# A guard on the weights that squares and sums every 16th column instead of all of them

## The chip, the core and the metric

The kernel runs on one core of a Trainium2 chip. The core has engines that run side by side, each through its own list of instructions in order: TensorE (PE in the profile) for matrix products, VectorE (DVE) and ScalarE (ACT) for work on tiles, GpSimd (POOL), and SyncE (SP), which here only issues DMAs. An engine that has to wait for another stands at a semaphore, and everything behind the waiting instruction in its list stands too. The metric is the device time of one execution in microseconds (us).

## What is computed

Two stages in a row. The first is a linear recurrence over 768 steps for 4 batches and 8 heads of width 48: a complex state, decayed by a gate of magnitude at most 0.999 at each step, takes up the outer product of k and v, and q reads it. The second takes the 3072 rows that come out (384 wide) through a two-layer network with 2048 hidden columns.

```python
mag = np.sqrt(a_re * a_re + a_im * a_im)
scale = np.minimum(mag, 0.999) / (mag + 1e-06)
a_re_n, a_im_n = (a_re * scale, a_im * scale)
for t in range(S):
    new_re = ar * S_re - ai * S_im
    new_im = ar * S_im + ai * S_re
    kv = np.einsum('bhd,bhe->bhde', k[:, :, t], v[:, :, t])
    S_re, S_im = (new_re + kv, new_im)
    y[:, :, t] = np.einsum('bhd,bhde->bhe', q[:, :, t], S_re)
...
h = x @ w_in
g = h - np.tanh(h)
return (g @ w_out).astype(np.float32)
```

## The kernel before

The sequence is cut into 6 chunks of 128 steps. A chunk of one batch is a unit (24 units), and two units are a group (12 groups, g = 0 to 11). For a group the kernel first computes the gates (`gates_b`, `gates_b2`, `gates_c`, `gates_d`, `gates_e`): logarithms and arctangents of the gate on ScalarE, sums over the 128 steps on TensorE (`cumsum`, lines 213 to 220), sines, cosines and exponentials on ScalarE. `products` (line 368) multiplies q and k with them (`qkf`, line 390), splits the result into a high and a low float16 part (`q`, `k`; the high part on ScalarE, line 400, the low part on VectorE, line 401) and transposes both by DMA (line 402). `attention` (line 424) makes the products within the chunk and with the carried state. The second stage works for a group as eight steps (fp = 0 to 7): `head` (line 513) has 18 matmuls into `h`, a tanh on ScalarE and a subtraction on VectorE into `mt`; `split` (line 531) makes a high part (ScalarE) and a low part (VectorE) of `mg`; `tail` (line 539) has 12 matmuls into `o`.

The arctangent in `gates_c` belongs to one set of ScalarE's function tables, logarithm and exponential to another, so each group loads tables (the rows named ACT_TABLE_LOAD, or ACT L102 with 1.28 us in the chain). After the arctangent, ScalarE writes the high part of the angle (`a_raw` in float16), and the first matmuls of `cumsum` (line 219) sum it.

The lists of the engines are not written out by hand. The strings START, FIRST, SECOND and CYCLE (lines 45 to 56) give the order in which the program's pieces are issued, for CYCLE in every group from g = 2; then a scheduler orders the instructions by priority and by its own estimate of when each can run and how long it takes. OFFSET and EARLY (lines 57 and 58) move the priority by kind. The guard's instructions have the kind "guard". Instructions of all helpers are recorded in `call` (line 102), so most rows of the profile have L102 and differ by their tile.

Beside the computation the kernel collects statistics that tell whether its fast path may be used (`stat`, line 131). For the weights it is `weight_stats` (line 193): for each of the 16 tiles of w_in and of w_out, one ScalarE instruction squares 384 columns of the high part and sums them per partition into a column of `stats`, and the square itself goes to a tile that nobody reads (`junk`). The sum is fetched by a second instruction, which the profile calls ACTIVATION_READ_ACCUMULATOR. The items w0 and w1 of SECOND and CYCLE call it, in `step` (lines 589 to 592). `check_stats` (line 556) compares all columns with limits at the end; they come from STAT_KINDS (line 70).

Of the kernel before, what the change touches and what calls it, by code (L numbers as in the profile page):

```python
# [13 lines left out]
AF = mybir.ActivationFunctionType  # L14
# [5 lines left out]
DM, DF = 384, 2048  # L20
# [5 lines left out]
FT = DF // P  # L26
# [47 lines left out]
    "o": (2 * NG - 2, -2.0 ** 100, 2.0 ** 100),  # L74
    "g": (FT // 2, 0.0, 2.0 ** 100),
    "x": (2 * NG, 14.0, 2.0 ** 30),
    "w": (2 * FT, 4.0, 2.0 ** 21.9),
}
STAT_COLS = {}
NSTAT = 0  # L80
# [6 lines left out]
def tile_fast(ctx: ExitStack, tc: tile.TileContext, flag, a_in, qkv_in, win_in, wout_in, sq_c, vec_c, lim_c, out):  # L87
    nc = tc.nc
    V, G, A, T, SP = nc.vector, nc.gpsimd, nc.scalar, nc.tensor, nc.sync
# [16 lines left out]
    V, G, A, T, SP = map(eng, (V, G, A, T, SP))  # L106
# [24 lines left out]
    def stat(kind, n=1):  # L131
        i = STAT_COLS[kind][used.count(kind)]
        used.extend([kind] * n)
        return stats[:, i:i + n]

    def junk():
        return sb.tile([P, 2 * HD], F16, name="junk")
# [32 lines left out]
    wi, wo = {}, {}  # L170
# [20 lines left out]
            combine("declo", "declo", out=t[:, 1], in0=w, in1=t[:, 0], op=ALU.subtract)  # L191

    def weight_stats(ft):
        A("guard").activation(out=junk()[:, :DM], in_=wi[ft][:, 0], func=AF.Square, accum_out=stat("w"))
        A("guard").activation(out=junk()[:, :DM], in_=wo[ft][:, 0], func=AF.Square, accum_out=stat("w"))


    gate = {}
# [382 lines left out]
    def step(g, x):  # L581
        kind, i = x[0], int(x[1:] or 0)
        if kind == "F":
            (gates_first, gates_second)[i]()
        elif kind == "q":
            load_qkv(i)
        elif kind in "io":
            decode(i, (0,) if kind == "i" else (1,))
        elif kind == "w":
            if 1 <= g <= FT // 2 and (kind, 2 * g + i) not in live:  # L590
                live[kind, 2 * g + i] = True
                weight_stats(2 * (g - 1) + i)
        elif kind in "pa":
            u = 2 * g + i
            if u < 2 * NG:
                advance(kind, u)
        elif g + i < NG and (kind, g + i) not in live:
            assert not any((kind, j) in live for j in range(g + i, NG))
            live[kind, g + i] = True
            steps[kind](g + i)  # L600
# [222 lines left out]
```

## Time and profile before

| what | value |
|---|---|
| runs without profile | 574.28, 575.5, 575.92 us; median 575.5 |
| profiled execution, own time | 575.09 us |
| its span, first to last instruction | 573.3 us |
| TensorE busy | 502.8 us, 88% of the span |
| VectorE busy | 475.2 us, 83% |
| ScalarE busy | 474.1 us, 83% |
| mean granted TensorE clock | 0.978 of full speed |

The span is shorter than the execution's own time by 1.8 us, which lie before its first and after its last instruction. The durations below come from this one execution. In the timelines a row has its start, its time, and in brackets the idle time before it with what ended it; an instruction on ScalarE or VectorE reaches some 0.1 us into the next one, so the distance between two starts is what it takes from its engine. In the chain of waits, each row is a piece of the time that ended last.

### The profile page before, as it was taken

Reading aid. Unit: us, or ns where it says so; the run is one execution under the profiler, and the core shown is the slowest. Engines: PE = TensorE matmul, PEld = TensorE weight load, DVE = VectorE, ACT = ScalarE, POOL = GpSimd, SP = SyncE. Lnnn points to the kernel's source line nnn. Section 1 sums busy time; section 2 is a strip of 40 time slices with the busy share of each in tenths; the row PEclk is TensorE's granted clock in tenths of the full one; section 3 lists DMA queues with packets and bytes.
Section 4 is the critical chain, followed back from the end, with each engine's and each line's share of the span. In section 5 each row is a group of like instructions: output and inputs, shape, how many; then the busy total and the mean of one; then the engine's idle time right before and its main releaser. Section 6 shows DMA issues by size and latency. Waiting matters only on the chain.

```text
span 573.3 us, 12669 instructions
## 1 busy us (share of the span) xinstructions
PE 502.8 (88%) x5058; PEld 385.8 (67%) x5058; DVE 475.2 (83%) x806; ACT 474.1 (83%) x951; POOL 2.3 (0%) x8
## 2 busy tenths in 40 slices
PE   2336499988879998999998999999999999999995
PEld 0135386856657766877776777778778777777773
DVE  4898899979799879898987998999998989853331
ACT  6978799897988978998988998998989989553551
POOL 1000000000000000000000000000000000000000
PEclk9998699999989999999998999999999999999999
DMA  7757834319675487176286285293482652720001
GB/s 248 212 167 173 267 111 125 112 20 203 120 125 145 74 129 172 45 147 154 56 153 143 49 183 143 59 182 106 99 179 67 136 110 57 147 58 15 4 25 33
DMA packets 133902, 68.12 MB, mean 119 GB/s; under 512 B 119982, under 2 KB 123694, under 8 KB 133836
## 3 DMA queue, kind: packets, MB, share of 16 engines
q1 hardware_dynamic: 133836, 67.25, 50.6%
q8 instruction: 41, 0.67, 0.5%
q14 instruction: 25, 0.20, 0.1%
HBM read 36.76 MB, written 4.78 MB: 72 GB/s over the span
## 4 chain that ended last, share of the span: by engine, by line
PE 34%; ACT 27%; DVE 22%; DMA 9%; issue 7%; SPq 1%; ACTq 0%; DVEq 0%
PE h L521 11%; PE o L548 10%; PE att L102 8%; ACT L102 5%; ACT a_raw L102 5%; DMA qT<-q 4%; DVE qkf L390 3%; DMA kT<-k 3%; DVE g_t L102 3%; ACT mg L102 3%; DVE qkv_raw L387 2%; DVE q L119 2%; ACT mt L102 2%; ACT g_t L102 2%; DVE mg L102 2%
## 5 line engine op out<-in xcount | busy, mean ns | idle before, releaser
L521 PE MATMUL h<-xT,w 128*128 128x256 f16 x1728 | 209.8, 275 | 13.5 <-DMA xT<-x 10.9
L548 PE MATMUL o<-w,mg 128*128 128x384 f16 x1152 | 204.3, 326 | 1.7 <-ACT mg L102 1.0
L521 PEld LDWEIGHTS <-w 128*128 128x128 f16 x1728 | 168.6, 99 | 43.9 <-DMA xT<-x 8.6
L548 PEld LDWEIGHTS <-mg 128*128 128x128 f16 x1152 | 111.3, 98 | 66.0 <-ACT mg L102 1.2
L102 DVE SCALAR_TENSOR_TENSOR mt<-h,mt 128x512 f32<-128x512 f32 x96 | 65.0, 688 | 28.6 <-ACT mt L102 27.7
L102 DVE SCALAR_TENSOR_TENSOR mg<-mt,mg 128x512 f16<-128x512 f32 x96 | 65.0, 687 | 17.4 <-ACT mg L102 16.5
L102 ACT ACTIVATE mt<-h 128x512 f32<-128x512 f32 x96 | 55.0, 587 | 24.5 <-PE h L521 24.4
L102 ACT ACTIVATE mg<-mt 128x512 f16<-128x512 f32 x96 | 59.1, 626 | 16.3 <-DVE mt L102 16.1
L102 ACT ACT_TABLE_LOAD x39 | 50.0, 1283 | 1.4 <-PEq L816 0.8
L102 PE MATMUL att<-qT,kT 96*128 96x128 f16 (+1 forms) x544 | 40.9, 228 | 4.1 <-DMA kT<-k 3.7
L390 DVE TENSOR_TENSOR qkf<-qkv_raw,g_trig 128x768 f32<-128x768 f32 x44 | 41.1, 952 | 0.0
L102 ACT ACTIVATE a_raw<-a_raw 128x768 f32<-128x768 f32 (+2 forms) x49 | 39.0, 798 | 0.5 <-DVE a_raw L102 0.4
L102 PEld LDWEIGHTS <-kT 96*128 96x128 f16 x480 | 29.3, 99 | 8.0 <-DMA kT<-k 4.6
L102 DVE TENSOR_TENSOR a<-af,a 128x512 f16<-128x512 f32 x40 | 27.2, 686 | 7.8 <-ACT a L102 7.7
L102 DVE TENSOR_TENSOR af<-att,sqc 128x512 f32<-128x512 f32 x40 | 27.3, 687 | 5.4 <-PE att L102 4.3
L102 ACT ACTIVATE a<-af 128x512 f16<-128x512 f32 x40 | 24.8, 623 | 3.7 <-DVE af L102 3.7
L102 DVE SCALAR_TENSOR_TENSOR g_t<-g_t,a_raw 128x768 f32<-128x768 f32 (+1 forms) x26 | 23.2, 897 | 2.3 <-ACT a_raw L102 2.3
L119 DVE TENSOR_TENSOR q<-qkf,q 128x768 f16<-128x768 f32 x20 | 19.1, 956 | 5.3 <-ACT q L102 5.3
L102 ACT ACTIVATE w<-wtmp 128x384 f16<-128x384 f32 x32 | 16.1, 518 | 8.4 <-DVE wtmp L186 8.4
L102 ACT ACTIVATE q<-qkf 128x768 f16<-128x768 f32 x20 | 16.9, 843 | 6.7 <-DMA qT<-q 6.4
L102 ACT ACTIVATE g_trig<-g_t 128x768 f32<-128x768 f32 (+1 forms) x26 | 20.4, 787 | 2.0 <-DVE g_t L102 2.0
L102 PE MATMUL att<-sqc,qkf 128*96 128x128 f32 x32 | 7.0, 386 | 16.2 <-DVE qkf L390 15.8
(94 smaller groups left out, 700.6 us busy)
## 6 DMA issues: line engine op xcount, KB each, us to landing
qkv_raw<-in_qkv SPq DMA_DIRECT2D x24, 576.0 KB
a_raw<-in_a SPq DMA_DIRECT2D x22, 384.0 KB
io<-in_win SPq DMA_DIRECT2D x16, 384.0 KB
io<-in_wout SPq DMA_DIRECT2D x16, 384.0 KB
out_dram<-io SPq DMA_DIRECT2D x24, 192.0 KB
a_raw<-in_a SPq DMA_DIRECT2D x4, 192.0 KB
xT<-x SPq DMA_TRANSPOSE x24
hd<-hscr SPq DMA_DIRECT2D x20, 3.0 KB
```

Of the source, the lines that this page charges most:

```text
L102: return f(*a, **k)
L119: by_name[ENGINE[which]](kind).tensor_tensor(**k)
L387: V("prod").scalar_tensor_tensor(out=x, in0=vw(e), scalar=E_MAX, in1=x, op0=ALU.min, op1=ALU.mult)
L390: V("prod").tensor_tensor(out=f, in0=x[:, :, None].broadcast_to([P, H, 2, D]), in1=tg[:, :, sl].rearrange("p r (h d) -> p h r d", d=D), op ...
L521: T("h").matmul(h_ps[:, j].rearrange("p (two t) -> p two t", two=2), lhsT=wi[ft][:, wp, kt * P:(kt + 1) * P], rhs=xT[:, :, xp, kt, :], sta ...
L548: T("o").matmul(o_ps[tt][:, :DM], lhsT=gg[:, gp, j * 256 + tt * P:j * 256 + (tt + 1) * P], rhs=wo[ft][:, wp], start=(ft == 0 and n == 0), ...
```

## The change

The two instructions of `weight_stats` read every 16th column of the tile, 24 instead of 384. The lower and the upper limit for these sums are divided by 16. The number of instructions stays the same.

```diff
@@ -74,7 +74,7 @@
     "o": (2 * NG - 2, -2.0 ** 100, 2.0 ** 100),
     "g": (FT // 2, 0.0, 2.0 ** 100),
     "x": (2 * NG, 14.0, 2.0 ** 30),
-    "w": (2 * FT, 4.0, 2.0 ** 21.9),
+    "w": (2 * FT, 4.0 / 16, 2.0 ** 17.9),
 }
@@ -191,8 +191,8 @@
     def weight_stats(ft):
-        A("guard").activation(out=junk()[:, :DM], in_=wi[ft][:, 0], func=AF.Square, accum_out=stat("w"))
-        A("guard").activation(out=junk()[:, :DM], in_=wo[ft][:, 0], func=AF.Square, accum_out=stat("w"))
+        A("guard").activation(out=junk()[:, :DM // 16], in_=wi[ft][:, 0].rearrange("p (n s) -> p n s", s=16)[:, :, 0], func=AF.Square, accum_out=stat("w"))
+        A("guard").activation(out=junk()[:, :DM // 16], in_=wo[ft][:, 0].rearrange("p (n s) -> p n s", s=16)[:, :, 0], func=AF.Square, accum_out=stat("w"))
```

Since the scheduler estimates the shorter instructions as shorter, it also puts other instructions in another order. ScalarE's list is shown where it works at the second unit of the group whose period runs from 302.6 to 343.9 us in the trace; `w_9` and `w_10` are weight tiles, `q` and `k` the high parts that line 400 writes.

```order
 L102 ACTIVATE junk,stats<-xf 128x384
 L102 ACTIVATE mt<-h 128x512 x2
-L102 ACTIVATE junk,stats<-w_9_719 128x384
-L102 ACTIVATE q_89<-qkf 128x8x96
-L102 ACTIVATE mg<-mt 128x512 x2
-L102 ACTIVATE junk,stats<-w_9_781 128x384
-L102 ACTIVATE mt<-h 128x512
-L102 ACTIVATE junk,stats<-w_10_431 128x384
-L102 ACTIVATE rawsq<-qkv_raw 128x144
-L102 ACTIVATE junk,stats<-w_10_912 128x384
+L102 ACTIVATE junk,stats<-w_9_719 128x24
+L102 ACTIVATE q_89<-qkf 128x8x96
+L102 ACTIVATE mg<-mt 128x512
+L102 ACTIVATE junk,stats<-w_9_781 128x24
+L102 ACTIVATE mg<-mt 128x512
+L102 ACTIVATE mt<-h 128x512
+L102 ACTIVATE junk,stats<-w_10_431 128x24
+L102 ACTIVATE rawsq<-qkv_raw 128x144
+L102 ACTIVATE junk,stats<-w_10_912 128x24
 L102 ACTIVATE mg<-mt 128x512
 L102 ACTIVATE mt<-h 128x512
```

On ScalarE only a guard instruction moved, between the two `mg`. VectorE's list at the same place reads so; `q_89` and `k_1_91` are the low parts of line 401, `qkv_raw` is the multiplication of line 387 and `qkf` that of line 390, both for k.

```order
 L102 SCALAR_TENSOR_TENSOR mt<-h,mt 128x512 x2
 L119 TENSOR_TENSOR q_89<-qkf,q_89 128x8x96
-L102 SCALAR_TENSOR_TENSOR mg<-mt,mg 128x512 x2
-L102 SCALAR_TENSOR_TENSOR mt<-h,mt 128x512
-L387 SCALAR_TENSOR_TENSOR qkv_raw<-g_en,qkv_raw 128x384
-L102 TENSOR_REDUCE stats<-rawsq 128x3
-L390 TENSOR_TENSOR qkf<-qkv_raw,g_trig 128x768
-L102 SCALAR_TENSOR_TENSOR mt<-h,mt 128x512
-L102 SCALAR_TENSOR_TENSOR mg<-mt,mg 128x512
+L102 SCALAR_TENSOR_TENSOR mg<-mt,mg 128x512
+L102 SCALAR_TENSOR_TENSOR mt<-h,mt 128x512
+L102 SCALAR_TENSOR_TENSOR mg<-mt,mg 128x512
+L387 SCALAR_TENSOR_TENSOR qkv_raw<-g_en,qkv_raw 128x384
+L102 SCALAR_TENSOR_TENSOR mg<-mt,mg 128x512
+L390 TENSOR_TENSOR qkf<-qkv_raw,g_trig 128x768
+L102 SCALAR_TENSOR_TENSOR mt<-h,mt 128x512
+L102 TENSOR_REDUCE stats<-rawsq 128x3
 L119 TENSOR_TENSOR k_1_91<-qkf,k_1_91 128x8x96
```

Ahead of `qkf` there stand now three `mg` and one `mt` in place of two `mg`, one `mt` and the small reduction, and the `mt` stands ahead of the second `mg`. The same block stands six times, once in each of the periods between 221.9 and 463.4 us. TensorE's list differs only further ahead, in its part up to about 210 us, and SyncE's at two places there; behind 466 us all lists are the same as before.

## Rows read from the trace of the kernel before

**Rows 1.** Busy time of each engine in two of the six periods between the loads of the arctangent's tables, and the sum over all six. Columns: stretch and its length, then busy time and count of TensorE, its weight loads, VectorE, ScalarE and GpSimd, the granted TensorE clock, the DMA engines' busy share, and GB/s.

```profile
261.50:302.60 41.10, 40.70 (x455) 31.75 (x454) 37.17 (x61) 37.12 (x75) 0.00 (x0) 1.00 0.55 118
302.60:343.90 41.30, 39.35 (x431) 30.38 (x429) 37.40 (x62) 37.26 (x77) 0.00 (x0) 0.96 0.56 121
...
sum 241.50, PE 234.97 PEld 182.80 DVE 223.32 ACT 221.83 POOL 0.00; mean PE 39.16 PEld 30.47 DVE 37.22 ACT 36.97 POOL 0.00
```

**Rows 2.** The waits of TensorE from 221.9 to 463.4 us, the only row of the answer: waiting line, releaser, us in total, times, longest.

```profile
PE att L219 <- ACT a_raw L102: 6.5, 6, 2.6
```

**Rows 3.** The chain of waits at the end of the period of 302.6 to 343.9 us: start, us, engine, tile and line.

```profile
340.38 0.88 DVE qkf L390
...
341.28 0.84 ACT k L102
342.13 0.52 ACT mg L102
342.65 0.48 ACT mt L102
343.13 0.73 ACT a_raw L102
...
343.88 1.28 ACT L102
...
345.81 0.74 ACT a_raw L102
```

**Rows 4.** The timeline of ScalarE in the same stretch, from a guard on the weights to the tanh ahead of `k`.

```profile
335.51 0.52 ACT L102 ACTIVATE junk<-w 128x384 f16<-128x384 f16 x1
...
336.06 0.85 ACT L102 ACTIVATE q<-qkf 128x768 f16<-128x768 f32 x1
336.81 1.14 ACT L102 ACTIVATE mg<-mt 128x512 f16<-128x512 f32 x2
337.85 0.51 ACT L102 ACTIVATE junk<-w 128x384 f16<-128x384 f16 x1
...
338.36 0.58 ACT L102 ACTIVATE mt<-h 128x512 f32<-128x512 f32 x1
```

**Rows 5.** The timeline of VectorE in the same stretch.

```profile
336.94 0.96 DVE L119 TENSOR_TENSOR q<-qkf,q 128x768 f16<-128x768 f32 x1
337.82 1.28 DVE L102 SCALAR_TENSOR_TENSOR mg<-mt,mg 128x512 f16<-128x512 f32 x2
339.02 0.68 DVE L102 SCALAR_TENSOR_TENSOR mt<-h,mt 128x512 f32<-128x512 f32 x1
339.62 0.55 DVE L387 SCALAR_TENSOR_TENSOR qkv_raw<-g_en,qkv_raw 128x384 f32<-128x384 f32 x1
340.08 0.30 DVE L102 TENSOR_REDUCE stats<-rawsq 128x3 f32<-128x144 f32 x1
340.30 0.95 DVE L390 TENSOR_TENSOR qkf<-qkv_raw,g_trig 128x768 f32<-128x768 f32 x1
341.20 0.69 DVE L102 SCALAR_TENSOR_TENSOR mt<-h,mt 128x512 f32<-128x512 f32 x1
```

**Rows 6.** Groups of ScalarE's instructions by tile and shape: count, busy us, mean ns of one, idle time before. `io<-io` is line 184, which reads every second 4-byte word.

```profile
L112 ACT ACTIVATE io<-io 128x384 f32<-128x384 f32 x32 | 16.8, 553 | 0.9 <-DVE wtmp L181 0.9
L102 ACT ACTIVATE junk<-w 128x384 f16<-128x384 f16 x32 | 16.5, 515 | 0.1
...
L102 ACT ACTIVATE rawsq<-qkv_raw 128x144 f32<-128x144 f32 x24 | 7.5, 312 | 0.6 <-DMA qkv_raw<-in_qkv 0.6
L102 ACT ACTIVATION_READ_ACCUMULATOR junk<-w 128x1 f32 x32 | 6.2, 192 | 0.0
```

**Rows 7.** The chain of waits around the first guard on weights, from the stretch of 100 to 185 us.

```profile
118.12 0.52 ACT junk L102 x2
...
118.66 0.62 ACT junk L102 x2
119.28 0.83 ACT a_raw L102
```

**Rows 8.** Three rows of ScalarE's timeline: the high part of the second unit's q, in the last period before 221.9 us and in two of the six.

```profile
214.08 0.84 ACT L102 ACTIVATE q<-qkf 128x768 f16<-128x768 f32 x1 [3.00 <-DMA qT<-q]
...
253.69 0.84 ACT L102 ACTIVATE q<-qkf 128x768 f16<-128x768 f32 x1
...
294.82 0.84 ACT L102 ACTIVATE q<-qkf 128x768 f16<-128x768 f32 x1 [1.43 <-DMA qT<-q]
```

**Rows 9.** Rows of TensorE's timeline: first sums of the angle (line 219) of four groups, the 12 matmuls behind two of them, and the last `h` ahead of the tanh of rows 3.

```profile
180.25 0.48 PE L219 MATMUL att<-a_raw,tri 128*128 128x384 f16 x2 [0.58 <-ACT a_raw L102]
...
224.61 0.48 PE L219 MATMUL att<-a_raw,tri 128*128 128x384 f16 x2 [2.58 <-ACT a_raw L102]
...
305.35 0.74 PE L219 MATMUL att<-a_raw,tri 128*128 128x384 f16 x2 [1.95 <-ACT a_raw L102]
305.89 1.49 PE L102 MATMUL att<-qT,kT 96*128 96x128 f16 x12
...
340.30 2.13 PE L521 MATMUL h<-xT,w 128*128 128x256 f16 x18
...
346.59 0.48 PE L219 MATMUL att<-a_raw,tri 128*128 128x384 f16 x2 [0.46 <-ACT a_raw L102]
346.92 0.83 PE L102 MATMUL att<-qT,kT 96*128 96x128 f16 x12
```

## The prediction, made before the changed kernel had run

> **What bounds the kernel now.** I read the busy times by period first. From 221.9 to 463.4 us the kernel repeats six times; the sum is 241.5 us, two periods take 41.1 and 41.3 us, and so the other four (241.5 - 82.4) / 4 = 39.8 us [rows 1]. TensorE is busy 39.2 us in a mean period (a few matmul records may be missing, so rather more), VectorE 37.2, ScalarE 37.0 [rows 1]: all three are nearly full, and their shares of the whole span don't tell which one sets the pace. So I read next who waits. TensorE waits in these six periods for one thing alone, the high part of the angle that ScalarE writes ahead of the sums of line 219: 6.5 us in six waits [rows 2]. Whatever the change does in this stretch, it does it by moving that point, and it cannot gain more there than 6.5 us.
>
> Then the chain shows what sets that point. In the period up to 343.9 us it runs through VectorE's `qkf` at 340.38, and then through ScalarE without a gap: the high part of k at 341.28, `mg`, a tanh, the arctangent at 343.13, the table load at 343.88 and the high part of the angle at 345.81; TensorE starts at 346.59 [rows 3, 9]. ScalarE had nothing left to do ahead of k: it waited for `qkf`. VectorE's timeline says why `qkf` isn't earlier: from 336.94 to 341.2 us its instructions stand end to end [rows 5]. So in front of k the pace is VectorE's, although the guards stand on ScalarE in just that stretch [rows 4].
>
> **What a guard costs, and what is saved.** A guard over 384 columns has 515 ns, and the row with 144 columns 312 ns: (515 - 312) / 240 = 0.85 ns a column [rows 6]. 360 columns fewer save 0.30 us, and leave some 0.21 us as a duration, near the 192 ns of the one-column read that follows [rows 6]; that read stays. 32 guards give 9.7 us of ScalarE's time. Bounds for one guard: nothing saved, if a column read at a distance of 32 bytes costs as much as 16 columns side by side, and 515 - 192 = 0.32 us, if it becomes as short as the one-column read. I take 0.30: the nearest row with a step, every second word, has 553 ns for 384 columns, 38 ns more than the guard [rows 6]. The Trainium skill (SBUF — State Buffer, section "Door 1: The DMA port swizzle") has a rule against this change: each access that goes to a new 16-byte line of SBUF pays a penalty, and here each column lies on a new line. By it the saving goes towards the lower bound, and the sum below would be up to 0.6 us higher; the row of line 184, with two words to a line, agrees in sign, with its 38 ns.
>
> **Where the saving shortens the path.** The first two guards stand in the chain, at 118.12 and 118.66, with the exponential right behind them at 119.28 [rows 7]. ScalarE runs end to end there, so both savings count: -0.6 us. The next four and the four after them lie in the periods that end with TensorE's waits of 0.58 and 2.58 us [rows 9], where several instructions change places. What can be gained is at most these waits, 3.2 us; what can be lost is what a later period loses (next part). Near 214 us ScalarE stands for 3.00 us before the high part of q, held by the transpose that reads the buffer [rows 8], and some tanh and `mg` now run in that hole; but `qkf` and k follow q at nearly the same distance, so I take a small gain, -0.3 us for each of the two, with bounds of -3.2 and +1.3 us together.
>
> **Where the new order lengthens it.** In each of the six periods VectorE has other work between the low part of q and `qkf`: one `mg` more, the reduction less. From start to start an `mg` takes 0.60 us (two from 337.82 to 339.02) and the reduction 0.22 (340.08 to 340.30) [rows 5]. So `qkf` moves back by 0.60 - 0.22 = 0.38 us. Also, `mt` now stands second. It needs its tanh, which on ScalarE comes after q (0.75 us), one `mg` (0.52), the guard (0.51 - 0.30 = 0.21) and another `mg` (0.52), and itself takes 0.58 [rows 4]: 336.06 + 2.58 = 338.64. VectorE would be ready at 337.82 + 0.60 = 338.42, so it stands 0.2 us more. Where the transpose lets q start earlier, by the 0.30 us of the guard ahead of it, this wait vanishes. Per period 0.4 to 0.6 us; behind `qkf` the list on ScalarE up to the angle is unchanged and without a gap [rows 3], so all of it arrives at TensorE, where the next `h`, and with it the next period, is late by as much. Six periods: 2.3 to 3.8 us; I take 0.5 each, 3.0 us. Behind ScalarE's k, low parts, transposes and the table load move back too, together, so nothing among them is newly late. The savings in these periods, 22 guards or 6.6 us, lie in the time in which ScalarE waits for `qkf` or for the transpose: they cost and bring nothing. If that cover went, because `qkf` came earlier, the next limit stands close: the tanh ahead of the arctangent needs an `h` that TensorE finishes at about 342.4 us, and it starts at 342.65 [rows 3, 9], so a perfect ScalarE would win some 0.3 us in that period.
>
> **The sum.** -0.6 - 0.3 - 0.3 + 3.0 = +1.8 us on the profiled execution's own 575.09 us, 576.9. The median of the runs is 0.4 us above it, so in the terms of the median 575.5 + 1.8 = 577.3 us. Its own range: 2.3 - 1.2 = +1.1 at the lower end, 3.8 with nothing gained ahead of it at the upper one, or 576.6 to 579.3 us. A measurement of this kernel tells about 0.3% (1.7 us) from no change, so the forecast lies right at that bound.
>
> **The rivals.**
>
> Hidden on both sides. The delay of `qkf` stays at the lower end, since q starts 0.3 us earlier wherever no transpose holds it (at 253.69 it started without a wait [rows 8]), and the rearranged periods ahead gain 1 us or so of their 3.2: 2.3 - 0.6 - 1.5 = +0.2 us, 575.7. For it speaks the 3.00 us hole near 214 us; against it that q at 294.82 follows a transpose and not the guard [rows 8].
>
> Faster, by a late transpose that comes in time. The two long periods lost 41.2 - 39.8 = 1.4 us each: in the first q stood 1.43 us for its transpose [rows 8], and then TensorE, after an idle time of 1.95 us, ran 12 matmuls in 1.49 us that take 0.83 elsewhere [rows 9], with a granted clock of 0.96 over the second period [rows 1]. If the other order lets this transpose land as early as in its neighbours, both go: 1.8 - 2.8 = -1.0 us; with the lower delay and 1 us more gained ahead, -2.7, or 572.8 to 574.5 us. It decides as soon as that q starts within 0.3 us of being ready. For it: the two places of SyncE's list that move lie ahead of these periods; against: SyncE's list within them is the same.
>
> Slower still, by the clock. TensorE now waits for the angle about 0.5 us longer in each period, some 1 us in most and 2.5 in one. If in two more periods the clock falls to its lower level of 1.2 GHz as it did behind the 1.95 us, the price is the 1.4 to 1.7 us of the second long period each, so 1.8 + 3.1 = +4.9 us, 580.4. Against it: the wait of 2.58 us at 224.61 ended with matmuls of 0.48 us, at full clock, while the same two took 0.74 behind the wait of 1.95 [rows 9]; the length of the wait alone did not decide. The Trainium skill (TensorE: Matmul & The Clock Gate, section "HAM oscillation") has the rule that idle gaps between bursts of matmuls bring the slower clock back each time; by it this rival would be likelier, and these two rows bear it out once in two.
>
> ScalarE sets the pace after all. Then the savings count where they stand, and TensorE's waits for ScalarE go: -0.6 - 6.5 = -7.1 us, 568.4. ScalarE's 83% and the releaser's name in rows 2 speak for it; against it that the chain passes through VectorE's `qkf` right ahead [rows 3].
>
> **How the numbers follow.** Forecast (577.3): 0.42, of which 0.34 above the bound of 577.2. Hidden: 0.28. Faster by the transpose: 0.14, of which 0.09 below 573.8. Slower by the clock: 0.10. ScalarE's pace: 0.06. So slower by over 0.3% has 0.34 + 0.10 = 0.44, faster 0.09 + 0.06 = 0.15, and the rest, 0.41, lies within. The range leaves out the last case, the lower third of the faster one and the upper half of the clock's: 573.8 to 580.0 us.
>
> **What the profile after will show.** A guard on weights of 0.20 to 0.22 us, and ScalarE's busy time near 464 us. The exponential behind the first two guards near 118.7 us. In the six periods VectorE's `qkf` of k starting 0.4 to 0.6 us later after the low part of q (3.7 to 4.0 us behind it in place of 340.30 - 336.94 = 3.36), and TensorE's waits at line 219 adding up to 6.5 + 3.0 = 9.5 us. If these waits are not longer than 6.5 us, the step on VectorE's order is wrong; if `qkf` is late and the waits are not, something else than k limits the angle. If the two long periods come down to 39.8 us, the transpose decided.

## The result, and the profile after

The changed kernel takes 580.54 us in the median of 16 runs (577.57 to 585.01), the kernel before 576.0 us (573.9 to 579.13) in the runs beside them: a ratio of 1.0084, with a 95% interval of 1.0063 to 1.0104. It is slower by 4.5 us, where +1.8 was forecast and 573.8 to 580.0 us was the range. The profiled execution took 581.99 us (before: 575.09). The page says of it:

```profile
span 580.2 us, 12664 instructions
...
PE 506.4 (87%) x5058; PEld 388.8 (67%) x5058; DVE 476.3 (82%) x806; ACT 466.2 (80%) x951; POOL 2.2 (0%) x8
...
PEclk9998699999889997999998999999999999999998
```

ScalarE works 7.9 us less and the span is 6.9 us longer. The guard and its read, in the groups by tile and shape (count, busy us, mean ns), answer to [rows 6]:

```profile
L102 ACT ACTIVATE junk<-w 128x24 f16<-128x24 f16 x32 | 7.5, 234 | 0.1
L102 ACT ACTIVATION_READ_ACCUMULATOR junk<-w 128x1 f32 x32 | 6.1, 190 | 0.0
```

The guard fell from 515 to 234 ns, the read stayed. Now the waits from 222.5 to 470 us, the six periods of the changed kernel; the first line answers to [rows 2]:

```profile
PE att L219 <- ACT a_raw L102: 10.1, 6, 3.6
...
ACT k L102 <- DVE qkf L390: 8.5, 6, 1.4
```

TensorE's waits for the angle grew from 6.5 to 10.1 us, and ScalarE stands in front of every `k`, 1.42 us each time, for VectorE's `qkf`. (The 6.5 us of rows 2, and the 10.1 us, hold the wait that ends the period before the six, 2.58 and 3.65 us, and not the one that ends the sixth; counted by period they are 4.8 and 8.2 us.) VectorE's timeline of one period, to be laid beside [rows 5]:

```profile
381.35 0.95 DVE L119 TENSOR_TENSOR q<-qkf,q 128x768 f16<-128x768 f32 x1
382.22 0.69 DVE L102 SCALAR_TENSOR_TENSOR mg<-mt,mg 128x512 f16<-128x512 f32 x1
383.09 0.69 DVE L102 SCALAR_TENSOR_TENSOR mt<-h,mt 128x512 f32<-128x512 f32 x1 [0.19 <-ACT mt L102]
383.70 0.68 DVE L102 SCALAR_TENSOR_TENSOR mg<-mt,mg 128x512 f16<-128x512 f32 x1
384.30 0.55 DVE L387 SCALAR_TENSOR_TENSOR qkv_raw<-g_en,qkv_raw 128x384 f32<-128x384 f32 x1
384.77 0.68 DVE L102 SCALAR_TENSOR_TENSOR mg<-mt,mg 128x512 f16<-128x512 f32 x1
385.37 0.95 DVE L390 TENSOR_TENSOR qkf<-qkv_raw,g_trig 128x768 f32<-128x768 f32 x1
```

From the low part of q to `qkf` it is 385.37 - 381.35 = 4.02 us, 3.36 before: the third `mg` in place of the reduction (0.38), and `mt`, which starts 0.87 us behind `mg` and not 0.60 (0.27). On ScalarE, in the same period:

```profile
380.47 0.84 ACT L102 ACTIVATE q<-qkf 128x768 f16<-128x768 f32 x1
...
384.35 0.58 ACT L102 ACTIVATE mt<-h 128x512 f32<-128x512 f32 x1
386.35 0.84 ACT L102 ACTIVATE k<-qkf 128x768 f16<-128x768 f32 x1 [1.42 <-DVE qkf L390]
387.10 0.61 ACT L102 ACTIVATE mg<-mt 128x512 f16<-128x512 f32 x1
387.62 0.58 ACT L102 ACTIVATE mt<-h 128x512 f32<-128x512 f32 x1
388.10 0.83 ACT L102 ACTIVATE a_raw<-a_raw 128x768 f32<-128x768 f32 x1
...
390.78 0.83 ACT L102 ACTIVATE a_raw<-a_raw 128x768 f16<-128x768 f32 x1
```

Between the starts of q and k lie 5.88 us. In rows 3 and 4 they are 341.28 - 336.06 = 5.22. The 0.66 us go through `mg`, `mt`, the arctangent and the table load to the angle, as they did in [rows 3], and so to TensorE. Its timeline shows that, and what follows the longest wait [rows 9]:

```profile
225.26 0.80 PE L219 MATMUL att<-a_raw,tri 128*128 128x384 f16 x2 [3.65 <-ACT a_raw L102]
225.86 1.48 PE L102 MATMUL att<-qT,kT 96*128 96x128 f16 x12
...
391.66 0.48 PE L219 MATMUL att<-a_raw,tri 128*128 128x384 f16 x2 [1.03 <-ACT a_raw L102]
391.98 0.83 PE L102 MATMUL att<-qT,kT 96*128 96x128 f16 x12
```

Behind the 3.65 us the same 12 matmuls take 1.48 us and not 0.83. The busy times of the stretch have the granted clock in the third column from the end, close to its lower level of 1.2 GHz:

```profile
225.30:231.20 5.90, 5.90 (x45) 4.73 (x45) 3.66 (x7) 2.67 (x6) 0.00 (x0) 0.52 0.85 209
```

All first sums of line 219, their waits, and the distance to the next one:

| before: start, wait | after: start, wait | distance before | after |
|---|---|---|---|
| 100.90, 1.03 | 101.42, 1.00 | 39.81 | 39.38 |
| 140.71, none | 140.80, none | 39.54 | 39.81 |
| 180.25, 0.58 | 180.61, none | 44.36 | 44.65 |
| 224.61, 2.58 | 225.26, 3.65 (half clock) | 39.60 | 42.70 |
| 264.21, 0.40 | 267.96, 0.86 | 41.14 | 41.74 |
| 305.35, 1.95 (half clock) | 309.70, 2.54 (half clock) | 41.24 | 41.74 |
| 346.59, 0.46 | 351.44, 1.11 | 39.92 | 40.22 |
| 386.51, 0.73 | 391.66, 1.03 | 39.60 | 40.13 |
| 426.11, 0.40 | 431.79, 0.95 | 40.02 | 40.92 |
| 466.13, 0.83 | 472.71, 1.74 | 107.2 to the end | 107.5 |

The six distances from 224.61 us are 5.93 us longer. Of these 2.66 us are the half clock: from the first sum to the last ten matmuls into `o` it is 231.19 - 225.26 = 5.93 us after and 227.88 - 224.61 = 3.27 before. The other 3.27 us, 0.55 a period, are left for the later k. Ahead of that, the profile after is 0.52 us late at 101 us already, where no guard on weights has run yet, and from there to 225 us it takes 123.84 us (123.71 before). The first distance is 0.43 us shorter, but it is 39.18 to 39.88 us in the other kernels with short guards below, and 39.32 in one with long guards and old lists (long, old, carry early), so no gain of the guards can be read from it.

### The profile page after: what moved, and what is told of

Read it like the earlier page. It is cut to its first block, busy times and chain, and to the rows that moved or that the text cites. A ratio compares the mean times of both kernels' runs of the same rounds, so it can differ in the third digit from the quotient of the medians.

```text
span 580.2 us, 12664 instructions
## 1 busy us (share of the span) xinstructions
PE 506.4 (87%) x5058; PEld 388.8 (67%) x5058; DVE 476.3 (82%) x806; ACT 466.2 (80%) x951; POOL 2.2 (0%) x8
## 4 chain that ended last, share of the span: by engine, by line
PE 33%; ACT 29%; DVE 19%; DMA 10%; issue 7%; SPq 1%; ACTq 0%; DVEq 0%
PE h L521 11%; PE o L548 10%; PE att L102 8%; ACT a_raw L102 5%; DMA qT<-q 4%; ACT L102 4%; DMA kT<-k 4%; ACT mg L102 3%; DVE qkf L390 2%; ACT mt L102 2%; ACT g_t L102 2%; DVE mt L102 2%; DVE g_t L102 2%; ACT q L102 2%; ACT k L102 2%
## 5 line engine op out<-in xcount | busy, mean ns | idle before, releaser
L102 PE MATMUL att<-qT,kT 96*128 96x128 f16 (+1 forms) x544 | 42.6, 233 | 4.8 <-DMA kT<-k 4.4
L102 PEld LDWEIGHTS <-kT 96*128 96x128 f16 x480 | 30.9, 102 | 9.2 <-DMA kT<-k 5.7
L102 ACT ACTIVATE k<-qkf 128x768 f16<-128x768 f32 x20 | 16.8, 840 | 8.8 <-DVE qkf L390 8.8
L219 PE MATMUL att<-a_raw,tri 128*128 128x384 f16 x40 | 11.1, 362 | 12.9 <-ACT a_raw L102 12.9
## 6 DMA issues: line engine op xcount, KB each, us to landing
qkv_raw<-in_qkv SPq DMA_DIRECT2D x24, 576.0 KB
```

The costliest lines, as they stand in the source:

```text
L102: return f(*a, **k)
L219: T("cum").matmul(c_ps[:, :HD], lhsT=tri, rhs=hl[:, bb, i], start=(i == 0), stop=(i == 1))
```

## The experiments

There were three theories. A: the guards' new length costs nothing, and the scheduler's new order costs what it puts ahead of `qkf` of k. B: the short guards themselves change the pace. C: the early part of the order, and TensorE's clock behind its longer waits, do it. An order was held by dependencies without a semaphore between instructions of one engine, so that its list reads as wanted and nothing else is added. A ratio below compares a kernel with the kernel before in the runs beside it; 0.001 is 0.58 us.

```diff
+    hold(tc)
...
+        tc.add_manual_dep(here[f"I-{then}"], f"I-{first}", mybir.DependencyInfo(mybir.DependencyClass.NoSync, mybir.DependencyReason.DATA), reason="order")
```

### Guard and order apart

Four kernels: short guards with all four lists of before; long guards with all lists of after; short guards with the new order from 221 us on only, and up to there only. Between the first two nothing but the guards' lines (here that of w_in), their limits and the order is exchanged:

```diff
-        A("guard").activation(out=junk()[:, :DM // 16], in_=wi[ft][:, 0].rearrange("p (n s) -> p n s", s=16)[:, :, 0], func=AF.Square, accum_out=stat("w"))
...
+        A("guard").activation(out=junk()[:, :DM], in_=wi[ft][:, 0], func=AF.Square, accum_out=stat("w"))
```

> The guards read 24 columns as in the change, but edges without a semaphore hold the lists of all engines in the order of the kernel before. Theory (the new order costs, the short guards cost nothing): TensorE's wait for the angle in the six periods falls back to its 4.8 us of before (0.40, 1.95, 0.46, 0.73, 0.40 and 0.83), the first guards bring 0.6 us, and the ratio to before is 0.997 to 1.000. Rival (the short guards with their step of 32 bytes disturb something by themselves, whatever the order): the ratio stays near 1.008. Rival (ScalarE sets the pace): 0.988 or less.

> The guards read all 384 columns as before, but the lists of all engines are held in the order of the changed kernel. Theory (the order costs): slower, ratio 1.008 to 1.011, a little over the changed kernel's 1.008, since the guards now also stand in the chain (0.6 us at 118 us, and up to 0.3 us per period where the tanh ahead of VectorE's second mt comes later). Rival (the short guards cost): ratio 0.999 to 1.001.

> Short guards; the lists are held in the order of before up to 221 us, and have the order of the change in the six periods behind. Theory (qkf of k later by 0.4 to 0.6 us in each period): waits of TensorE for the angle 3 us longer in sum than before, the matmuls behind the wait at 225 us at full clock again, ratio 1.003 to 1.006. Rival (the part up to 221 us with its fall of the clock made the loss): ratio 0.998 to 1.001.

> Short guards; the lists have the order of the change up to 221 us, and are held in the order of before in the six periods behind. Theory: the wait at 225 us stays about 3.6 us and with it the half clock behind it (2.7 us), the six periods have their length of before: ratio 1.002 to 1.005. Rival (the order up to 221 us costs nothing by itself, the clock fell for another reason): 0.998 to 1.001.

| run | median us | ratio, interval | q to k, us |
|---|---|---|---|
| short guards, old order | 575.75 | 1.0006 (0.9982 to 1.0030) | 5.22 |
| long guards, new order | 583.35 | 1.0146 (1.0117 to 1.0175) | 6.23 |
| short, new in the six periods | 579.75 | 1.0074 (1.0047 to 1.0101) | 5.88 |
| short, new ahead of them | 578.33 | 1.0032 (1.0002 to 1.0062) | 5.22 |

The last column is the usual distance between the starts of ScalarE's q and k of a second unit in the six periods, as in the timeline above. The short guards alone change nothing that the interval tells, some 1.4 us either way; B falls. The order costs, most of it in the six periods, and with long guards it costs still more: there the instructions that VectorE waits for come later, and k is 1.01 us late. Two of these runs came out slower than any theory had them: 1.0146 and 1.0074, where at most 1.011 and 1.006 were expected. The two halves of the order add up to 6.1 us over the kernel before, the changed kernel's own ratio gives 4.8; each has some 1.2 to 1.7 us of uncertainty.

### The two differences ahead of `qkf`

VectorE's block, with the `mt` ahead of the second `mg` (and with it ScalarE's guard between its two `mg`, as in the changed kernel), or with the third `mg`, each alone. Here and below, lists are shortened to the names of the tiles:

```diff
  q, mg
- mg, mt, qkv_raw, reduction, qkf
+ mt, mg, qkv_raw, reduction, qkf
```

```diff
  q, mg, mg, mt, qkv_raw
- reduction, qkf, mt, mg
+ mg, qkf, mt, reduction
```

> Short guards; all lists as in the kernel before, but in the six periods VectorE's mt stands ahead of the second mg, and ScalarE's guard between its two mg, as in the changed kernel. The third mg and the reduction stay where they were. So of the two differences that the forecast priced, only the second is left (0.02 to 0.22 us a period), and the 0.38 us of mg against reduction are gone. Theory (each difference costs what it puts ahead of qkf): 575.75 us of the run with all lists in the old order, plus 0.1 to 1.3: 575.9 to 577.1. Rival (the early mt itself does the harm, since VectorE and ScalarE now wait for one another in turn): near the 579.7 of the run with the new order in the six periods.

> The counterpart of the run with mt ahead of the second mg: short guards, all lists as before, but in the six periods the third mg stands ahead of qkf and the reduction behind it; mt and the guard on ScalarE stay where they were. Theory (what VectorE has ahead of qkf is added to the way from ScalarE's q to its k, and this to each period): q to k 5.22 + 0.38 = 5.60 us, six times 0.38 = 2.3 us above 575.75: 578.0. So far the runs with 5.22, 5.49 and 5.89 us from q to k had 575.75, 577.44 and 579.75 us. Rival (the two differences only cost together, or the third mg saves behind qkf what it costs ahead of it): within 1 us of 575.75.

Measured: 577.44 us (1.0015, 0.9992 to 1.0037) with k 0.27 us later (5.49), and 579.42 us (1.0055, 1.0028 to 1.0081) with k 0.71 us later (5.93). The third `mg` alone costs more than the 0.38 us of its place, and VectorE's timeline says why:

```profile
340.19 0.54 DVE L387 SCALAR_TENSOR_TENSOR qkv_raw<-g_en,qkv_raw 128x384 f32<-128x384 f32 x1
340.97 0.69 DVE L102 SCALAR_TENSOR_TENSOR mg<-mt,mg 128x512 f16<-128x512 f32 x1 [0.23 <-ACT mg L102]
341.58 0.95 DVE L390 TENSOR_TENSOR qkf<-qkv_raw,g_trig 128x768 f32<-128x768 f32 x1
```

It stands for ScalarE's `mg`, which itself waits 0.41 us for VectorE's `mt`; in the full new order `mt` is earlier, and that wait is gone (384.77 above). So the two don't add: 0.27 and 0.71 alone, 0.66 together. As far as the runs tell, k's lateness and the time go together: six times 0.27, 0.66 and 0.71 us are 1.6, 4.0 and 4.3 us, and the ratios above the old order's come to 0.5, 3.9 and 2.8 us, each with some 2 us of uncertainty. So A stands for the six periods, though no closer than that.

### Is it the angle alone?

If k costs by way of the angle, an earlier angle pays. First by 0.9 us, with the high part ahead of the table load, in the old and the new order:

```diff
  ScalarE: k, mg, mt, arctangent
- table load, mg, a_raw (f16)
+ a_raw (f16), table load, mg
  VectorE: k, mg
- mt, carry, mg, a_raw (f16)
+ carry, a_raw (f16), mt, mg
```

> Short guards, all lists in the order of the kernel before, except that behind the arctangent of each of the six periods the high part of the angle is written ahead of the table load and of one mg on ScalarE (before: behind both), and VectorE adds the carry and takes the low part two instructions earlier. Theory (TensorE's wait for the angle at line 219 sets the pace): the angle comes 0.9 us earlier, the six waits of 0.40, 1.95, 0.46, 0.73, 0.40 and 0.83 us shrink by up to 0.9 each, 3.7 us in all: 572.0 us, and below that if the half clock behind the wait of 1.95 us goes too. Rival (the angle only happens to come last; another limit stands right behind it): within 1 us of 575.75.

> The changed kernel with its own lists, and the same early angle as in the other run of this call. Theory (the new order costs time only by way of the angle): its waits of 0.86, 2.54, 1.11, 1.03, 0.95 and 1.74 us shrink by 0.9 each, some 5.3 us, so 580.5 becomes 575.2, and what is left above the run in the old order is the early part with the clock behind the wait of 3.65 us (1.8 us by the run with only that part new) and up to 1.5 us. Rival (the order costs on other ways too): still 4 to 5 us above the run in the old order.

Slower: 580.51 us (1.0079, 1.0054 to 1.0105) and 592.41 (1.0241, 1.0188 to 1.0294). The runs of the second lie 11 us apart, so only the sign is used; 575.2 or some 580 us were expected of it, and what makes it so long isn't shown. TensorE's waits in the six periods of the first, and VectorE's:

```profile
PE att L102 <- DVE af L102: 8.0, 5, 1.8
PE att L219 <- ACT a_raw L102: 3.7, 2, 2.7
```

```profile
347.21 0.96 DVE L102 SCALAR_TENSOR_TENSOR a_raw<-a_raw,a_raw 128x768 f16<-128x768 f32 x1 [0.91 <-ACT a_raw L102]
348.08 0.68 DVE L102 SCALAR_TENSOR_TENSOR mt<-h,mt 128x512 f32<-128x512 f32 x1
349.46 0.69 DVE L102 SCALAR_TENSOR_TENSOR mg<-mt,mg 128x512 f16<-128x512 f32 x1 [0.70 <-ACT mg L102]
```

The waits at line 219 are gone in five of six periods, as meant, and 8.0 us of waits for VectorE's `af` stand right behind five of them, with a sixth of 1.76 us behind the window: VectorE now waits 1.6 us in this period, first for the angle and then for `mg` (0.43 us before, for `mg` alone), and ScalarE's early angle itself stands 1.01 us for the carry that VectorE adds. TensorE's wait named the angle, but right behind it VectorE is the next to be late. So a milder form, in which nobody stands much longer than before:

```diff
  ScalarE: arctangent, table load
- mg, a_raw (f16)
+ a_raw (f16), mg
  VectorE: k, mg
- mt, carry, mg, a_raw (f16)
+ carry, mt, a_raw (f16), mg
```

> Short guards, all lists as before, but behind the arctangent of the six periods VectorE adds the carry one instruction earlier (ahead of mt) and takes the low part of the angle ahead of its last mg, and ScalarE writes the high part right behind the table load, ahead of its mg. The milder form of the early angle that cost 4.8 us: there VectorE stood 0.9 us for the angle and 0.7 us for mg in each period. Theory (TensorE's wait for the angle is worth its length, as long as no other engine stands for it): angle 0.5 us earlier, up to 0.5 us of each of the six waits of 0.4 to 2.0 us, 575.75 - 2.6 = 573.1. Rival (VectorE's list is the bound behind the angle as well, so whatever comes earlier is stood out there): 575.2 to 576.3, or slower if VectorE stands longer than before.

> The kernel before with its guards of 384 columns and its lists, but with the carry and the angle earlier in the six periods, as in the run of 574.47 us. It tells whether that gain needs the short guards. Theory (the guards lie where ScalarE waits, so their length is worth nothing with this order either): 574 to 575. Rival (the short guards gain as soon as TensorE's wait for the angle is gone): 576 and above.

> Short guards, the new order in the six periods only (579.75 us), and in them the carry and the angle earlier, as in the run of 574.47 us. Theory (the later k costs by way of the angle alone, 0.67 us a period): the early angle takes back at most 0.5 us of it in each period, 3 us: 576.8. Rival (the later k holds up VectorE's own list too): 578.5 and above, 4 us and more over the run in the old order.

With short guards it took 574.47 us (0.9973, 0.9946 to 1.0000), with long ones 575.41 (0.9978, 0.9954 to 1.0002), in the new order 578.56 (1.0042, 1.0020 to 1.0065). The first has this in the six periods:

```profile
PE att L219 <- ACT a_raw L102: 4.0, 2, 2.5
PE att L102 <- DVE af L102: 1.9, 5, 0.4
```

The 4.0 us hold the wait of 2.55 us ahead of the six periods; at their ends the waits for the angle fell from 4.8 to 1.4 us, and 2.3 us came back at `af`, 0.38 in each of the six (the last lies behind the window). Against the short guards in the old order the gain is 1.3 us by the medians and 1.9 by the ratios, where 2.6 were the most expected. These first two are the only kernels with a ratio below 1, and at the edge of what their intervals tell. Long guards do as well within the intervals, so no worth of the guards' length shows in this order either. The third stands at its rival's number, though the early angle gains as much in the new order (1.8 us by the ratios) as in the old. How much of this is TensorE's waiting shows in its waits at the ends of the six periods, for the angle and for `af`, from one profile each, beside the time, both as a difference from the short guards in the old order (4.8 us of waits; the time by the ratios, of 576 us):

| run | waits, us | more waits | more time |
|---|---|---|---|
| short, `mt` first | 6.2 | 1.4 | 0.5 |
| short, new in the six periods | 7.8 | 3.0 | 3.9 |
| short, third `mg` | 8.5 | 3.7 | 2.8 |
| short, old, angle earliest | 1.1 + 9.8 | 6.1 | 4.2 |
| short, old, carry early | 1.4 + 2.3 | -1.1 | -1.9 |
| long, old, carry early | 2.3 + 2.3 | -0.2 | -1.6 |
| short, new in the six, carry early | 5.7 + 2.3 | 3.2 | 2.1 |

The rows agree within 0.8 to 1.9 us, no closer than the 2 us of uncertainty of each time. With the early part in the time, which alone is 1.5 us by this count, the changed kernel has 3.4 us more waits and 4.5 us more time, and the long guards in the new order 6.1 and 8.1. TensorE's work is the same in all of them, so that time follows its waits is near to bookkeeping; that the order is the cause is shown by the exchange of the lists. What the table adds is the place: the order costs what TensorE waits longer, at the angle or right behind it, and a move that only shifts the wait from one to the other wins nothing.

### The clock behind TensorE's waits

Matmuls that nobody needs fill the waits: 22 and 15 in the changed kernel at 225 and 310 us, and 18 at 224 us in the kernel with the new order only ahead of 221 us.

```diff
-    def cumsum(hl, bb, which):
+    def cumsum(hl, bb, which, fill=0):
...
-        for i in range(2):
-            T("cum").matmul(c_ps[:, :HD], lhsT=tri, rhs=hl[:, bb, i], start=(i == 0), stop=(i == 1))
+        for i in range(-fill, 2):
+            T("cum").matmul(c_ps[:, :HD], lhsT=tri, rhs=wi[0][:, 0] if i < 0 else hl[:, bb, i], start=(i <= 0), stop=(i != 0))
```

> The changed kernel with its own lists, and matmuls that nobody needs right ahead of line 219 in two periods: 22 where TensorE waited 3.65 us at 225 us, and 15 where it waited 2.54 us at 310 us, at about 0.16 us each 3.5 and 2.4 us. Nothing starts earlier by them. Theory (TensorE's clock falls to its lower level behind the idle time, and the matmuls of the next 6 us pay for it): no fall at these two places, so 2.7 and 0.7 us less than 580.5: 577.1. Rival (the clock falls for another reason, or the time behind the waits is not TensorE's): no change, 580 to 581, or up to 0.5 more where the fillers outlast the wait.

> The kernel with the new order only up to 221 us, and 18 matmuls that nobody needs where TensorE waited 3.05 us at 221 to 224 us. Without them that kernel took 578.33 us, with a granted clock under 0.970 in 10 of 12 runs, and the one with all lists in the old order 575.75 us with 5 of 12. Theory (the new order of the early part costs nothing but a fall of the clock behind the longer wait): the fall goes, most runs have 0.970 and more, and the time is within 1 us of 575.75. Rival (it costs by its transposes and what they hold up): 577.5 to 579.5, whatever the clock. The matmuls behind the fall took 2.7 us more than at full clock, so that is also the most that can be won.

Measured 582.91 us (1.0110, 1.0076 to 1.0144) and 579.03 (1.0046, 1.0020 to 1.0072): nothing is won. TensorE's timeline of the first shows that the fillers did what they should:

```profile
223.29 3.74 PE L219 MATMUL att<-w,tri 128*128 128x384 f16 x22
226.87 0.49 PE L219 MATMUL att<-a_raw,tri 128*128 128x384 f16 x2
227.19 0.83 PE L102 MATMUL att<-qT,kT 96*128 96x128 f16 x12
```

Full clock behind the place, and the next first sum follows 267.22 - 226.87 = 40.35 us later (42.70 without). The first three periods are 4.3 us shorter than in the changed kernel's profile, and the last three give 2.3 us of it back: ScalarE's q waits there 1.04, 0.48 and 1.74 us for its transpose, and the waits at line 219 are 1.93, 1.37 and 2.63 us. So 2.05 us are left in the six periods of this profile, but it is 1.49 us late at the first sum near 102 us, ahead of all fillers, and the median shows no gain. In the second, another wait stands right where the half clock was:

```profile
224.77 0.48 PE L219 MATMUL att<-a_raw,tri 128*128 128x384 f16 x2 [0.65 <-ACT a_raw L102]
...
228.83 0.84 PE L102 MATMUL att<-qT,kT 96*128 96x128 f16 x12 [1.29 <-DMA kT<-k]
```

The transpose of k isn't there yet. So the half clock is real in a profile, 2.7 us, but in these two profiles part of what it delayed was late anyway, and no run shows that the time comes back with the clock.

### The early part and SyncE's list

> The kernel with the new order only up to 221 us, but SyncE's list is the old one: the load of qkv_raw is issued again ahead of hd and xT, and not right ahead of the transposes of q and k that the period up to 224 us waits for. Theory (the early part costs by those transposes, which the load pushes back): back to within 1 us of 575.75, and the transpose of q at 208 us lands as in the kernel before. Rival (it costs by the order on ScalarE and VectorE, and the transposes only follow): still 578 to 579.

```diff
  SyncE: hscr
- xT transpose, hd, hd, qkv_raw load
+ qkv_raw load, hd, hd, xT transpose
```

579.10 us (1.0048, 1.0025 to 1.0071), as with SyncE's new list: putting the load back wins nothing. The waits between 182 and 231 us, of SyncE and of TensorE:

```profile
SPq L102 <- DVE qkf L390: 2.8, 1, 2.8
```

```profile
PE h L521 <- DMA xT<-x: 2.8, 1, 2.8
```

The load stands until VectorE's `qkf` has read the buffer, and with the old list a transpose stands behind it, for which TensorE then waits 2.8 us. It is issued 209.57 - 182.64 = 26.9 us behind the first sum of line 219, and was 203.83 - 180.25 = 23.6 us behind it in the kernel before. So this run has a wait of its own in place of the one at the angle, and the load follows VectorE's `qkf`. On ScalarE, in the changed kernel, the list has `mg` directly ahead of k:

```profile
214.81 0.84 ACT L102 ACTIVATE q<-qkf 128x768 f16<-128x768 f32 x1 [2.54 <-DMA qT<-q]
219.61 0.63 ACT L102 ACTIVATE mg<-mt 128x512 f16<-128x512 f32 x1 [1.78 <-DVE mt L102]
220.48 0.84 ACT L102 ACTIVATE k<-qkf 128x768 f16<-128x768 f32 x1 [0.23 <-DVE qkf L390]
```

q to k is 5.67 us here, and 5.67 in the kernel with only this part new (before: 219.30 - 214.08 = 5.22 by the same view). But in that kernel the first sum at 224.27 us comes no later for it: it follows the one before in 44.09 us, 44.36 before. What is longer there is the next distance, 42.37 us against 39.60, at half clock behind a wait of 3.05 us. Since the fillers took that away and the time stayed, the cause of the early part's 1.5 to 1.8 us stays open.

### The guard alone

```diff
-        A("guard").activation(out=junk()[:, :DM // 16], in_=wi[ft][:, 0].rearrange("p (n s) -> p n s", s=16)[:, :, 0], func=AF.Square, accum_out=stat("w"))
...
+        A("guard").activation(out=junk()[:, :DM // 16], in_=wi[ft][:, 0, :DM // 16], func=AF.Square, accum_out=stat("w"))
...
```

> The changed kernel, but the guard reads the first 24 columns of a tile, side by side, and not every 16th; the lists are the same. It measures the guard alone. If a column at a distance of 32 bytes costs more than its neighbour, the guard falls from 232 ns to 205 to 215 ns (the line through the rows with 144 and 384 columns gives 210); if the distance costs nothing, 225 to 235 ns stay. For the time no theory expects a difference that one run can tell.

This guard covers other columns than the reference of the change; only its duration is used. The rows of the tile, min/median/max in ns:

```profile
L102 ACT ACTIVATE junk<-w x32: 204/210/223, 119.9 to 464.3; 128x24 f16<-128x24 f16 x32
```

210 ns, as the line through the two older rows gave; the distance of 32 bytes costs the 22 ns up to the 232 ns (median) of the changed kernel, about 1 ns a column.

## Why the prediction was wrong

The mechanism that lengthens the path was right, in its place and its sign: the scheduler's order, and in it VectorE's list ahead of `qkf`. What failed are the step on the first two guards, the term of the two rearranged periods, and the size of the six periods. The sum's own upper end had 3.8 us for the six and nothing lost ahead of them; 4.0 and 0.6 came.

- **The first two guards, -0.6.** This step failed. "ScalarE runs end to end there, so both savings count" was read from a chain that names only what came last. VectorE's `g_t`, for which the exponential of rows 7 also waits, was done 0.07 us ahead of that exponential. Before:

```profile
117.30 0.83 ACT L102 ACTIVATE a_raw<-a_raw 128x768 f32<-128x768 f32 x1
...
119.19 0.92 ACT L102 ACTIVATE a_raw<-g_t,vec 128x768 f32<-128x768 f32 x1
...
118.16 0.96 DVE L102 SCALAR_TENSOR_TENSOR g_t<-g_t,a_raw 128x768 f32<-128x768 f32 x1 [0.43 <-ACT a_raw L102]
```

After, ScalarE stands there:

```profile
117.82 0.83 ACT L102 ACTIVATE a_raw<-a_raw 128x768 f32<-128x768 f32 x1
...
119.67 0.93 ACT L102 ACTIVATE a_raw<-g_t,vec 128x768 f32<-128x768 f32 x1 [0.43 <-DVE g_t L102]
```

From one to the other it is 1.85 us, and was 1.89: 0.04 us gained, not 0.6.

- **The two rearranged periods, -0.3 each.** The profile has +0.27 and +0.29, and the run with only that order new is 1.8 us slower than the kernel before. "`qkf` and k follow q at nearly the same distance" was wrong: in the second of them k is 0.45 us later behind q. Whether that is what took the gain away isn't shown.
- **The six periods, 0.5 each, 3.0.** VectorE's delay is 0.38 + 0.27 = 0.65 us in the example, above the forecast's 0.4 to 0.6; from the low part of q to `qkf` the six periods have 3.85 to 4.26 us, 4.02 in the mean, where 3.7 to 4.0 were foretold. The bound that the wait for `mt` vanishes where q starts earlier did not come true: beyond the 0.38 us of the third `mg` there are 0.11 to 0.52 us in each of the six. Six times 0.66 are 4.0 us; the run with this part alone has 1.0074, or 4.3 us.

So 0.0 + 0.3 + 0.3 + 4.0 = 4.6 us by these sizes, and 4.5 were measured. That they meet so closely is partly luck: the sizes are those of one profile, whose 2.66 us of half clock they leave out, and the distances up to 225 us differ by more than 0.3 us between profiles of like kernels.

The rivals: "hidden on both sides" and "the late transpose" didn't happen; q still stood 1.65 us for its transpose at 298.50 (1.43 before). "ScalarE sets the pace" falls with the run in the old order. "Slower still, by the clock" came within 0.1 us of the time, at 580.4, but that is luck for the most part. In the profile the half clock costs 2.7 us (1.4 to 1.7 foretold) behind the wait of 3.65, where before the wait had been 2.58 and the clock full. Of the 16 runs of the changed kernel 12 had a mean granted clock below 0.970, of 98 runs of the kernel before 45; but below it the medians are 581.9 and 577.4 us, and at 0.970 and more 579.1 (4 runs) and 575.5, so at like clock 3.6 to 4.5 us of difference stay. The mean of a run doesn't tell where its clock fell, either: it is 0.956 in the profile with the fillers, where the clock is full at both filled places and 0.50 to 0.77 in every 10 us from 20 to 80 us, ahead of the first guard on weights (without fillers, 0.67 to 0.80 from 50 to 80 us). So the order carries most of the difference, and filling the wait didn't bring the time back.

Of the signs, the guard is 0.23 us (0.20 to 0.22 foretold), ScalarE's busy time 466.2 (464), the exponential didn't come earlier, and the waits are 10.1 us (9.5). The Trainium skill (SBUF — State Buffer, section "Door 1: The DMA port swizzle") has an access to a new 16-byte line pay a penalty; the 22 ns for 24 columns at a distance of 32 bytes agree with it in sign.

## What to carry to other kernels

A cheaper instruction can make a scheduled kernel slower: the saving lay where its engine waited, and the scheduler, which counted with it, moved others ahead of the instruction that all wait for; hold the old order to tell the two apart. Before a saving in the chain is counted, look for the second-latest input of the next instruction, here 0.07 us earlier than the latest. And a wait that names an engine is worth its length only if the engines behind that wait have time to take it: 0.9 us of earlier angle cost 4.8 us by the medians, and 0.5 us, with a list in which nobody stood much longer, won 1.3, at the edge of what the runs tell.

## What the runs showed of the hardware that was not expected

TensorE's clock is not told by the length of a wait alone. Behind 3.05, 3.33, 3.43 and 3.65 us at 224 to 227 us the first two sums took 0.80 us, but behind 3.14 us at 310 us, with long guards in the new order, they took 0.48, and the granted clock was 1.00 over the whole stretch:

```profile
310.31 0.48 PE L219 MATMUL att<-a_raw,tri 128*128 128x384 f16 x2 [3.14 <-ACT a_raw L102]
...
304.00:318.00 14.00, 10.86 (x148) 8.76 (x147) 12.14 (x21) 11.59 (x22) 0.00 (x0) 1.00 0.63 143
```

Behind 2.54 to 2.67 us at 224 to 227 us they took 0.48 us in most profiles, but 0.80 behind 2.64 us in the run with the old order, and with the new order in the six periods the clock fell about a microsecond later: behind 2.58 us the first two sums took 0.48 and the next two 0.78. Elsewhere 2.68 us at 308 us was followed by 0.48 with the third `mg`, and 1.95 us at 305 us by 0.74 in the kernel before. The Trainium skill (TensorE: Matmul & The Clock Gate, section "HAM oscillation") has idle gaps bring the slower clock back; most of the longest waits agree, the 3.14 us don't, and the middle ones go both ways.
